# Strassen's seven products for the first layer of the last two experts, weight tiles in one pool, logit penalties in pairs

## The chip, the cores and the metric

The kernel runs on one core of a Trainium2 chip. The metric is device microseconds (us) of one execution of the whole program, as a median over runs; one further execution was profiled. PE is the matrix engine (PEld its weight loads), DVE the vector engine, ACT the scalar engine, POOL the general engine whose queue also issues the indirect DMAs, SP the engine that issues plain DMAs.

## What is computed

```python
X = np.fft.rfft(x, axis=1)                      # x: 8 x 2496 x 256
y = np.fft.irfft(X * (filt_r + 1j*filt_i), n=2496, axis=1)
x = y.reshape(19968, 256)
logits = x @ w_gate                             # 8 experts
# greedy: over all (token, expert) in falling order of logit, a token takes the expert
# if it has none yet and the expert has fewer than 19968/8 = 2496 tokens
for e in range(8):
    h = np.maximum(x[mask_e] @ w1[e], 0.0)      # 256 -> 1024
    out[mask_e] = h @ w2[e]                     # 1024 -> 256
```

## The kernel before

The program has two parts. First the filter: transforms by matmuls, up to about 440 us; it writes the rows x to DRAM (`xs`) and keeps the logits in `lg`. Then the experts, from 448 us on. Which expert is served in which order is found by `Route`: eight phases, each of which fixes one more expert and its 2496 tokens (`phase`, `threshold`, `counts`), lists them (`places`) and so allows the weights of that expert to be loaded (`Ffn.weights`, indirect DMAs issued by POOL, L804) and its rows to be gathered (`Ffn.gather`, L823). While PE works on one expert, DVE, ACT and a few small matmuls (L567, L580, L764) work on the route of the next one. After each phase the logits of served experts are pushed down by `pen`: eight activations on ACT, one per expert, at L727.

**Precision.** Matmuls take fp32r operands. A value is held as a rounded high part and a low part, the rest; a product is made of three matmuls (high by high, high by low, low by high). The parts come from `nc.scalar.copy` (high) and a DVE subtraction (low): for weights in `split` (L816, L817; tiles `w0h`, `w0l`, `w1`), for the gathered rows in `turn` (L840, L841; tiles `xo`, `z`).

**One expert.** `Ffn.run` takes 2496 tokens in five groups g of 512 (the last has 448). First layer, `first(g, f)`: for each of 8 column blocks f of the weights, six matmuls of 512 columns into one PSUM bank `pz` (L859), 48 a group; then a ReLU on ACT (L865) for the high part and a `scalar_tensor_tensor` on DVE (L873, L876 in the last group, POOL at L869 in some) for the low part, both into a tile `hl`. Second layer, for each of four blocks t of 128 tokens: 8 pairs of matmuls, 512 and 256 columns (L913, L914), into `py`; then a copy on ACT (L923), an addition on POOL (L924) and an indirect DMA to `out` (L925). The last block of an expert has 64 tokens and takes 16 matmuls of 256 columns (L909). The second layer of group g and the first layer of group g + 1 alternate (`ORD`). `turn` makes the transposed rows of the next group from eight matmuls by a unit matrix (L837) in passing.

**Order of the work.** PE's order is the order of the program text (`manual_schedule`). For the other engines a scheduler in the compiler orders the instructions by its own model of time, so an instruction of ACT or DVE can stand earlier or later in its queue than in the text. Each engine's queue is then worked off in that order. The route is put between the matmuls by `Pump`: the matmul code yields an amount of time (`yield 0.65` for a quarter of a second layer), `Pump.feed` adds it to a clock, and a step of the route is written when its lag has passed. `pump.limit` says which phase may finish.

PSUM has eight banks: two for the route (`a`), two for `py` (`b`), four for `pz` and the transposes (`c`).

Of the kernel before, what the change touches and what calls it, by code (L numbers as in the profile page):

```python
# [7 lines left out]
F32, F32R = mybir.dt.float32, mybir.dt.float32r  # L8
# [8 lines left out]
S = B * G  # L17
CAP = N
# [8 lines left out]
V1, V1D, V2, V3, VP, I2, AC = 8, 0.5, 3, 2, -1, 5, 6.5  # L27
NP, NZ, MZ, NXO, ZB, NH = 5, 4, 8, 4, 2, 10

# [440 lines left out]
class Route:  # L470
# [10 lines left out]
    def setup(s):  # L481
# [34 lines left out]
        nc.gpsimd.memset(s.r[:, :8], float(CAP))  # L516
        s.tmp = t("tmp", [117, S, 8])
        s.iota, s.sidx = t("iota", [117, 512], F16), t("sidx", [128, 20])
        io = s.tmp.rearrange("p s e -> p (s e)")[:, :512]
        nc.gpsimd.iota(io, [[1, 512]], base=0, channel_multiplier=0, allow_small_or_imprecise_dtypes=True)  # L520
# [116 lines left out]
    def phase(s, ph):  # L637
# [22 lines left out]
        s.want()  # L660
        vc, need, tot, mem = v("vc", [128, 1]), v("need", [128, 1]), v("tot", [117, 4]), v("m0", [117, S])
        tb, pf = v("tb", [117, 2], F16), v("pf", [117, 4])
# [6 lines left out]
        if ph < 7:  # L669
# [14 lines left out]
            nc.vector.scalar_tensor_tensor(q, s.desc, vc, r1[:, :8], op0=OP.is_equal, op1=OP.mult, accum_out=need)  # L684
            ga, eqm, cum = v("ga", [117, S]), v("eqm", [117, S]), v("cum", [117, S])
            nc.vector.scalar_tensor_tensor(ga, s.M, T[:117, :1], s.ar, op0=OP.is_gt, op1=OP.mult)
# [37 lines left out]
        if ph == 7:  # L724
            return
        for e in range(8):
            nc.scalar.activation(s.lg[:, :, e], s.lg[:, :, e], AF.Identity, bias=pen[:117, e:e+1], scale=1.0)  # L727
        with s.tc.issue_after(s.last):
            t, t3 = v("u", [117, S]), v("u2", [117, S])
            nc.vector.scalar_tensor_tensor(s.asg, mem, 50.0, s.asg, op0=OP.mult, op1=OP.add)  # L730
# [53 lines left out]
class Ffn:  # L784


    def __init__(s, tc, i, xs, out, cp, ww, zp, ps):
        s.tc, s.nc, s.xs, s.out, s.ww, s.zp, s.ps = tc, tc.nc, xs, out, ww, zp, ps
        s.w1 = i['w1l']
        s.w2 = i['moe_w2'].rearrange("e (q f) d -> (e q) (f d)", f=8)  # L790
        s.id = cp.tile([128, 128], F32, name="id")
        make_identity(s.nc, s.id)
        s.scat = []
        s.wt, s.xg, s.xT = {}, {}, {}

    def weights(s, e, widx):
        nc = s.nc
        raw = [s.ww.tile([128, 2048], F32, name=f"wr{k}", bufs=1) for k in range(2)]
        off = bass.IndirectOffsetOnAxis(ap=widx[:, :1], axis=0)
        hl = [[s.ww.tile([128, 2048], F32R, name=f"w0{h}", bufs=2) for h in 'hl']]  # L800
        s.w2b = s.ww.tile([128, 2, 2048], F32R, name="w1", bufs=2)
        hl.append([s.w2b[:, k] for k in range(2)])
        s.wt[e] = (raw, hl, s.w2b)
        s.load = lambda k: nc.gpsimd.indirect_dma_start(out=raw[k], out_offset=None, in_=(s.w1, s.w2)[k], in_offset=off).ins  # L804

    def split(s, e, part):

        nc = s.nc
        raw, hl, _ = s.wt[e]
        k, h = divmod(part, 4)  # L810
        src, (hi, lo) = raw[k], hl[k]
        if k == 0:
            h, j = divmod(h, 2)
            h += 2 * j
        src, hi, lo = (t[:, 512*h:512*h+512] for t in (src, hi, lo))
        nc.scalar.copy(hi, src)  # L816
        nc.vector.tensor_tensor(lo, src, hi.bitcast(F32), op=OP.subtract)  # L817

    def gather(s, e, g, ids):
        for t in range(4*g, 4*g + 4):  # L820
            n = min(128, CAP - 128*t)
            xg = s.xg[e, t] = s.wp.tile([128, D], F32, name="xg", bufs=8)
            s.lastg = s.nc.gpsimd.indirect_dma_start(out=xg[:n], out_offset=None, in_=s.xs,  # L823
                                           in_offset=bass.IndirectOffsetOnAxis(ap=ids[0][:n, t:t+1], axis=0)).ins

    def turn(s, e, g, h):
# [14 lines left out]
        return nc.vector.tensor_tensor(lo, p[:, :, :w], hi.bitcast(F32), op=OP.subtract).ins  # L841

    def run(s, e, pump, hook):

        nc = s.nc
        ids = pump.out[e]
        out_rows = s.out
        _, ((w1h, w1l), (w2h, w2l)), w2 = s.wt[e]
        hs = {}

        def first(g, f):
# [4 lines left out]
            for k in range(2):  # L856
                sl = slice(1024*k+128*f, 1024*k+128*f+128)
                for w, x in ((w1h, xh), (w1h, xl), (w1l, xh)):
                    nc.tensor.matmul(p[:, :n], w[:, sl], x[:, k, :n], start=m == 0, stop=m == 5)  # L859
                    m += 1  # L860
                yield 0.65 * n / 512
            hl = s.wp.tile([128, 1024], F32R, name="hl", bufs=NH)
            hs.setdefault(g, []).append(hl)
# [14 lines left out]
        def firsts(g, count):  # L878
            for f in range(len(hs.get(g, ())), min(8, len(hs.get(g, ())) + count)):
# [7 lines left out]
                yield from first(g, f)  # L887

        hook(('g', 1))
        for g in range(5):  # L890
            n = min(512, CAP - 512*g)
            yield from firsts(g, 8)
            if g == 4:
                hook('last')
            if g == 0:
                hook('w2')
            for t in range(4):
                if g < 4:
                    yield from firsts(g + 1, ORD[t])
                w = min(128, n - 128*t)  # L900
                half = w == 64
                pp = s.ps.tile([128, 2, D], F32, name="py", tag="b", bufs=2)
                p = pp[:, 0]
                hi, lo, both = slice(128*t, 128*t+w), slice(512+128*t, 512+128*t+w), slice(384, 512)
                m = 0
                for f in range(8):
                    if half:
                        for a, b in ((both, w2h), (hi, w2l)):
                            nc.tensor.matmul(p[:a.stop-a.start], hs[g][f][:, a], b[:, 256*f:256*f+256],  # L909
                                             start=m == 0, stop=m == 15, skip_group_check=True)  # L910
                            m += 1
                    else:
                        nc.tensor.matmul(pp, hs[g][f][:, hi], w2[:, :, 256*f:256*f+256], start=f == 0, stop=False, skip_group_check=True)  # L913
                        nc.tensor.matmul(pp[:, f % 2], hs[g][f][:, lo], w2h[:, 256*f:256*f+256], start=False, stop=f > 5, skip_group_check=True)  # L914
                    if f in ((3,) if half else (1, 3, 5)):
                        yield 0.65
                yy = s.wp.tile([128, 2, D], F32, name="y", bufs=4)
                y = yy[:, 0]
                if half:
                    nc.scalar.copy(y[:w], p[w:])  # L920
                    nc.vector.tensor_tensor(y[:w], p[:w], y[:w], op=OP.add)
                else:
                    s.lasta = nc.scalar.copy(yy, pp).ins  # L923
                    nc.gpsimd.tensor_tensor(y, y, yy[:, 1], op=OP.add)  # L924
                st = nc.gpsimd.indirect_dma_start(  # L925
                    out=out_rows, out_offset=bass.IndirectOffsetOnAxis(ap=ids[1][:w, 4*g+t:4*g+t+1], axis=0),
                    in_=y[:w], in_offset=None)
                for o in s.scat:
                    s.tc.declare_no_dep(st.ins, o.ins, reason="each token has one place")
                s.scat.append(st)  # L930
                if t in (1, 2) and g == 4:
                    hook(t)
                yield 0.65


def emit(tc, i, out):
    nc = tc.nc
    with ExitStack() as st:
# [52 lines left out]
        def weights(e):  # L991
            W.weights(e, pump.out[e][2])
            W.load(0)
            if e:
                R.wdma = W.load(1)
            split.extend((e, p) for p in range(8))
        pump.on_w = weights
# [19 lines left out]
        zst.close()  # L1017
        W.wp = pool(st, "ffp", reuse_waits="tile")
        def gather(e, g):
            pump.until((e, g))  # L1020
            W.gather(e, g, pump.out[e])
# [11 lines left out]
        n = 0  # L1033
# [4 lines left out]
        with tc.manual_schedule(engines={mybir.EngineType.PE}):  # L1038
            for e in range(8):
                pump.limit = e + 1  # L1040
                def hook(what):
                    if what == 'w2':
                        flush(8)
                    elif isinstance(what, tuple):
                        gather(e, what[1])
                    elif e < 7:
                        if what == 'last':
                            gather(e + 1, 0)
                            flush(4)
                        else:  # L1050
                            W.turn(e + 1, 0, what - 1)
                for pe in W.run(e, pump, hook):
                    pump.feed(pe)
# [91 lines left out]
```

## Time and profile before

| what | us |
|---|---|
| median of 3 runs | 1469.07 |
| lowest and highest run | 1453.58, 1471.03 |
| the profiled execution | 1465.58 |
| its span, first to last instruction | 1463.8 |

The profiled execution lies 1.8 us above its span and 3.5 us below the median; the three runs are 17 us apart. The mean granted PE clock of the span was 0.982. A row's duration of a matmul has the time through the array in it, so matmuls that follow each other overlap: the time that one costs is read as the distance of two starts.

### The profile page before, as it was taken

The page shows a single profiled execution, that of the slowest core. Times are in us where ns is not written, and L with a number is a line of the kernel's source. Part 1 is how long each engine was busy: PE and PEld are TensorE (multiplying, and loading weights), DVE is VectorE, ACT ScalarE, POOL GpSimd, SP SyncE. Part 2 cuts the span into 40 slices and gives each one's busy share as a digit, 9 for nine tenths or more (in the row PEclk, how much of TensorE's full clock was granted, in tenths as well). Part 3 has the DMA queues.
Part 4 walks back from the last instruction along what each step waited for, and adds up shares of the span by engine and source line. Part 5 has one row for each costly group of instructions (what it writes and reads, how often), then busy time and mean ns, then how long its engine had stood idle before and what let it go on. Part 6 is the DMA issues. An engine that isn't in the chain of part 4 may idle for free. (4 is left out here: it accounts for less than half of the span.)

```text
span 1463.8 us, 24844 instructions
## 1 busy us (share of the span) xinstructions
PE 1391.3 (95%) x9127; PEld 1148.7 (78%) x9127; DVE 955.6 (65%) x2574; ACT 723.7 (49%) x1686; POOL 663.6 (45%) x729
## 2 busy tenths in 40 slices
PE   7899999998997999899999899999999999999998
PEld 6889899776445787677778788787878888888887
DVE  5666676576566789666876976977877854432231
ACT  5666677534473345344544533644553654533332
POOL 5433344243004745553664546366545644445423
PEclk9999999999998999999999999999999999999999
DMA  8554454888892102112110211211211221111100
GB/s 263 185 148 143 126 163 116 237 239 206 328 348 74 51 22 95 53 35 75 59 52 25 98 49 39 90 51 48 95 37 50 102 95 52 38 48 46 42 26 27
DMA packets 54780, 149.17 MB, mean 102 GB/s; under 512 B 9258, under 2 KB 29866, under 8 KB 50706
## 3 DMA queue, kind: packets, MB, share of 16 engines
q0 software_dynamic: 17552, 57.72, 12.1%
q1 hardware_dynamic: 9803, 47.11, 10.6%
q10 hardware_dynamic: 27304, 42.76, 9.5%
q8 instruction: 72, 1.18, 0.3%
q14 instruction: 49, 0.40, 0.1%
HBM read 83.89 MB, written 63.70 MB: 101 GB/s over the span
## 5 line engine op out<-in xcount | busy, mean ns | idle before, releaser
L913 PE MATMUL py<-w,hl 128*128 128x512 f32 x1216 | 445.6, 405 | 0.5 <-ACT hl L865 0.3
L914 PE MATMUL py<-w,hl 128*128 128x256 f32 x1216 | 341.9, 281 | 1.0 <-DVE hl L873 0.6
L865 ACT ACTIVATE hl<-pz 128x512 fp32r<-128x512 f32 (+1 forms) x320 | 186.8, 586 | 214.7 <-PE pz L859 189.0
L859 PE MATMUL pz<-xo,w0h 128*128 128x512 f32 (+1 forms) x640 | 264.4, 413 | 10.3 <-DVE hl L876 3.7
L913 PEld LDWEIGHTS py<-w,hl 128*128 128x128 f32 x1216 | 229.8, 189 | 51.4 <-issue 1.2
L924 POOL TENSOR_TENSOR y<-y 128x256 f32<-128x256 f32 x152 | 122.4, 806 | 311.2 <-ACT y L923 309.9
L859 PE MATMUL pz<-xo,w0l 128*128 128x512 f32 (+1 forms) x640 | 249.9, 390 | 0.0
L859 PE MATMUL pz<-z,w0h 128*128 128x512 f32 (+1 forms) x640 | 249.3, 390 | 0.2 <-issue 0.2
L914 PEld LDWEIGHTS py<-w,hl 128*128 128x128 f32 x1216 | 230.7, 190 | 5.3 <-DVE hl L873 2.2
L873 DVE SCALAR_TENSOR_TENSOR hl<-pz,hl 128x512 fp32r<-128x512 f32 x227 | 155.0, 687 | 116.0 <-ACT hl L865 101.8
L823 POOL DMA_INDIRECT xg<-xs,xid x160 | 168.3, 1052 | 135.8 <-issue 41.0
L923 ACT COPY y<-py 128x512 f32<-128x512 f32 x152 | 89.1, 586 | 282.8 <-PE py L914 188.5
L925 POOL DMA_INDIRECT out<-y,oid x160 | 174.5, 1090 | 48.1 <-POOL y L924 33.6
L859 PEld LDWEIGHTS pz<-xo,w0h 128*128 128x128 f32 x640 | 122.0, 191 | 33.7 <-DVE hl L873 3.8
L232 POOL TENSOR_TENSOR P<-P 128x256 f32<-128x256 f32 x80 | 58.9, 737 | 184.6 <-DVE P L230 184.5
L859 PEld LDWEIGHTS pz<-xo,w0l 128*128 128x128 f32 x640 | 121.3, 190 | 24.1
L859 PEld LDWEIGHTS pz<-z,w0h 128*128 128x128 f32 x640 | 122.0, 191 | 17.3 <-DVE z L841 1.0
L216 ACT COPY Y<-p 64x240 f32<-64x240 f32 (+1 forms) x304 | 116.0, 382 | 30.4 <-PE p L209 19.8
L209 PE MATMUL p<-cS,xr 117*128 117x120 f32 x688 | 100.5, 283 | 7.2 <-DMA xr<-xl 7.1
L559 DVE TENSOR_TENSOR Gm<-M,thr 117x1232 bf16<-117x1232 f32 (+2 forms) x80 | 105.5, 1329 | 0.2
L209 PEld LDWEIGHTS p<-cS,xr 117*128 117x128 f32 x688 | 91.0, 199 | 11.2 <-issue 4.7
L224 PE MATMUL p<-cW,Y 128*128 128x128 f32 x640 | 88.7, 281 | 2.3 <-ACT Y L216 1.5
(229 smaller groups left out, 2274.2 us busy)
## 6 DMA issues: line engine op xcount, KB each, us to landing
zd<-zt ACTq DMA_DIRECT2D x80, 256.0 KB
z<-zd SPq DMA_DIRECT2D x18, 600.0 KB
xs<-xo ACTq DMA_DIRECT2D x18, 600.0 KB
xr<-xl SPq DMA_DIRECT2D x6, 1404.0 KB
xr<-xl SPq DMA_DIRECT2D x7, 1111.5 KB
xr<-zd SPq DMA_DIRECT2D x8, 600.0 KB
xs<-xr ACTq DMA_DIRECT2D x8, 600.0 KB
xs<-Y ACTq DMA_DIRECT2D x6, 600.0 KB
```

The costliest lines, as they stand in the source:

```text
L209: nc.tensor.matmul(p[:, q-q0, :120], s.xr[b][:, q], s.cS1, start=True, stop=True)
L216: x = (nc.vector.tensor_copy if dve else nc.scalar.copy)(dst, src)
L559: nc.vector.tensor_tensor(Gm[:, s0:s1, :m], s.M[:, s0:s1].unsqueeze(2).to_broadcast([117, s1 - s0, m]), thr[:117].unsqueeze(1).to_broadcas ...
L823: s.lastg = s.nc.gpsimd.indirect_dma_start(out=xg[:n], out_offset=None, in_=s.xs, in_offset=bass.IndirectOffsetOnAxis(ap=ids[0][:n, t:t+1] ...
L859: nc.tensor.matmul(p[:, :n], w[:, sl], x[:, k, :n], start=m == 0, stop=m == 5)
L865: s.lasta = nc.scalar.activation(h[:, :n], p[:, :n], AF.Relu).ins
L873: nc.vector.scalar_tensor_tensor(l[:, :n], p[:, :n], 0.0, h[:, :n].bitcast(F32), op0=OP.max, op1=OP.subtract)
L913: nc.tensor.matmul(pp, hs[g][f][:, hi], w2[:, :, 256*f:256*f+256], start=f == 0, stop=False, skip_group_check=True)
L914: nc.tensor.matmul(pp[:, f % 2], hs[g][f][:, lo], w2h[:, 256*f:256*f+256], start=False, stop=f > 5, skip_group_check=True)
L923: s.lasta = nc.scalar.copy(yy, pp).ins
L924: nc.gpsimd.tensor_tensor(y, y, yy[:, 1], op=OP.add)
L925: st = nc.gpsimd.indirect_dma_start(out=out_rows, out_offset=bass.IndirectOffsetOnAxis(ap=ids[1][:w, 4*g+t:4*g+t+1], axis=0), in_=y[:w], i ...
```

## The change

1. **Experts 6 and 7** (`E0 = 6`) take their first layer by Strassen's algorithm. A group's product (weights 1024 x 256, rows 256 x 512) is split in two on each of its three axes. Seven products of half size take the place of eight: `11·b11`, `12·b21`, `s1·t1`, `s2·t2`, `s3·t3`, `s4·b22`, `22·t4`, where s1 to s4 are sums of weight quarters and t1 to t4 sums of row quarters. Each is again three matmuls, now of 256 columns. `step` does half of the output columns (d), so a group has 2 x 42 matmuls. Sums of products are made in PSUM: a bank is copied into another by ACT (L939), DVE adds into a bank (L945) or to SBUF (L949), and matmuls go on accumulating in it.
2. `sums` makes the seven weight operands, `turns` the seven row operands.
3. `run7` takes the place of `run` for these experts: after each of four parts of a step come two quarters of the second layer of the group before (`s.pend`), which is held over from group to group and from expert to expert. Eight matmuls of ones (L1059) stand at the end of expert 5's first layers; the last group has 512 columns with zero rows (a `memset` of `xg`).
4. Weights of all experts lie in tiles `w0` of one size, 16 of them (before: `w0h`, `w0l` and `w1`, two each). `hl` (10) becomes `ha` (5) and `hb` (6). Some route tiles have one buffer instead of two.
5. After every second of the eight activations of `pen` there is a `yield`, and after phase 6 they are left out.
6. The yields of the second layer are 0.7 (0.45 in the block of 64) instead of 0.65.

```diff
+E0 = 6
...
-        for e in range(8):
+        if ph == 6:
+            yield 'd', 0.5
+        for e in range(8 if ph < 6 else 0):
             nc.scalar.activation(s.lg[:, :, e], s.lg[:, :, e], AF.Identity, bias=pen[:117, e:e+1], scale=1.0)
+            if e % 2 == 1 and e < 7:
+                yield 'd', 1.4
...
+    def sums(s, e):
+
+        r11, r21, r12, r22 = (s.wt[e][0][0][:, 512*h:512*h+512] for h in range(4))
+        tt = s.nc.vector.tensor_tensor
+        s.halve(*s.block(e, '11'), r11)
+        s1 = s.ww.tile([128, 1024], F32, name="w0", bufs=16)[:, :512]
+        tt(s1, r21, r22, op=OP.add)
+        yield
+        s.halve(*s.block(e, 's1'), s1)
+        tt(r21, r21, r11, op=OP.subtract)
+        yield
+        tt(r11, s1, r11, op=OP.subtract)
+        s.halve(*s.block(e, 's2'), r11)
+        yield
+        s.halve(*s.block(e, '12'), r12)
+        tt(r12, r12, r11, op=OP.subtract)
...
+        p = bank(0)
+        nc.scalar.copy(f[:, 0:4:3], p.rearrange("p (k c) -> p k c", c=256))
...
+        p = bank(1)
+        nc.scalar.copy(f[:, 1], p[:, 256:])
+        tt(f[:, 0], p[:, :256], f[:, 0], op=OP.subtract)
+        tt(f[:, 2], p[:, :256], f[:, 1], op=OP.subtract)
+        u2, u4 = tile(), tile()
+        s.halve(u4[:, 0, :256], u4[:, 1, :256], p[:, 256:])
+        tt(f[:, 1], f[:, 1], f[:, 0], op=OP.subtract)
+        s.halve(u2[:, 0], u2[:, 1], s.scr[:, :512])
+        tt(f[:, 3], f[:, 3], f[:, 1], op=OP.subtract)
...
+        p11, pm = bank(), bank()
+        prods((p11, '11', 'b11', True), (pm, 's1', 't1', True))
+        pu = bank()
+        nc.scalar.copy(pu, p11)
+        m5, c22 = (s.wp.tile([128, 512], F32, name="hr", bufs=2) for _ in range(2))
+        nc.scalar.copy(m5, pm)
+        yield 1.42
+        prods((pu, 's2', 't2', False), (p11, '12', 'b21', False))
+        p12 = bank()
+        nc.vector.tensor_tensor(p12, pu, m5, op=OP.add)
+        relu(p11, 0, 0)
+        yield 1.42
+        prods((pu, 's3', 't3', False), (p12, 's4', 'b22', False))
+        nc.vector.tensor_tensor(c22, pu, m5, op=OP.add)
+        yield 1.42
+        relu(p12, 1, 0)
+        relu(c22, 1, 1)
+        prods((pu, '22', 't4', False))
+        relu(pu, 0, 1)
+        yield 0.71
...
+                ps = [s.ps.tile([128, 512], F32, name="pz", tag="c", bufs=4) for _ in range(4)]
+                for n, m in ((512, True), (1, False)):
+                    for p in ps:
+                        nc.tensor.matmul(p[:, :n], s.ones16[:117], s.iota[:, :n], start=m, stop=True, skip_group_check=True)
...
-                    if f in ((3,) if half else (1, 3, 5)):
-                        yield 0.65
+            if m in (1, 3, 5):
+                yield 0.45 if half else 0.7
```

On ACT, in the route's third phase, these rows stand around the eight activations of `pen` (L727) before; `pz` banks are ReLUed into `hl`, `py` copied to `y`, `ptr` holds transposed rows:

```order
L923 COPY y_7831<-py_7795 128x512
L865 ACTIVATE hl_7890<-pz_7883 128x512
L923 COPY y_7910<-py_7893 128x512
L727 ACTIVATE lg_69<-lg_69,pen_7881 117x176 x8
L865 ACTIVATE hl_7921<-pz_7914 128x512
L840 CAST xo_7924<-ptr_7926 128x2x256
L865 ACTIVATE hl_7940<-pz_7933 128x512
```

In the changed program the activations of the same phase are at L731:

```order
L1016 ACTIVATE hb_8003<-pz_7996 128x512
L1016 ACTIVATE ha_8013<-pz_8006 128x448
L731 ACTIVATE lg_69<-lg_69,pen_7978 117x176 x3
L982 COPY y_8034<-py_8017 128x512
L731 ACTIVATE lg_69<-lg_69,pen_7978 117x176 x5
L982 COPY y_8073<-py_8050 128x512
```

One copy stands between three and five of them; in the phase after, one copy between one and seven, and in the second, fifth and sixth phase all eight follow each other, as before.

On PE, in the first group of expert 6, a bank of the first layer before is:

```order
L909 MATMUL py_14651<-w1_12366,hl_14560 64x256
L859 MATMUL pz_14680<-xo_14614,w0h_13829 128x512
L859 MATMUL pz_14680<-z_14615,w0h_13829 128x512
L859 MATMUL pz_14680<-xo_14614,w0l_13830 128x512
L859 MATMUL pz_14680<-xo_14614,w0h_13829 128x512
L859 MATMUL pz_14680<-z_14615,w0h_13829 128x512
L859 MATMUL pz_14680<-xo_14614,w0l_13830 128x512
```

In the changed program this is the second half (d = 1) of that group, and the start of the next group; products `11`, `s1`, `s2`, `12`, `s3`, `s4`, `22` in this order, six matmuls each:

```order
L925 MATMUL pz_14806<-z_14626,w0_14522 128x256 x6
L890 MATMUL ptr_14824<-id_4814,xg_14649 128x128 x2
L890 MATMUL ptr_14824<-id_4814,xg_14651 128x128 x2
L925 MATMUL pz_14819<-z_14626,w0_14527 128x256 x6
L925 MATMUL pz_14805<-xo_14615,w0_14530 128x256 x6
L890 MATMUL ptr_14853<-id_4814,xg_14653 128x128 x2
L890 MATMUL ptr_14853<-id_4814,xg_14655 128x128 x2
L925 MATMUL pz_14819<-z_14634,w0_14534 128x256 x6
L925 MATMUL pz_14848<-xo_14627,w0_14537 128x256 x6
L925 MATMUL pz_14819<-z_14634,w0_14540 128x256 x6
L925 MATMUL pz_14917<-z_14830,w0_14517 128x256 x6
L925 MATMUL pz_14918<-xo_14861,w0_14522 128x256 x6
```

The second layer of expert 5 is used up by then and that of this group needs both halves, so only transposes stand between the products here; in every later group quarters of a second layer stand there.

On DVE, at the same place, the queue before has a ReLU's low part, a low part of weights or rows, and the route in turn:

```order
L817 TENSOR_TENSOR w0l_14689<-wr0_14686,w0h_14688 128x512
L841 TENSOR_TENSOR z_14734<-ptr_14735,xo_14733 128x2x256
L873 SCALAR_TENSOR_TENSOR hl_14751<-pz_14742,hl_14751 128x512
L765 TENSOR_TENSOR loc_14698<-sidx_3687,rt_14758 128x2
L873 SCALAR_TENSOR_TENSOR hl_14768<-pz_14754,hl_14768 128x512
L817 TENSOR_TENSOR w0l_14689<-wr0_14686,w0h_14688 128x512
L841 TENSOR_TENSOR z_14734<-ptr_14771,xo_14733 128x2x256
```

In the changed program, from the addition into p12 (L945) on; `wr0_14938` is the raw first-layer weight of expert 7, `w0_15434` and the like its operands, `tmp` the scratch of the row sums:

```order
L945 TENSOR_TENSOR pz_14848<-pz_14819,hr_14821 128x512
L897 TENSOR_TENSOR z_14830<-tmp_3685,z_14830 128x512
L816 TENSOR_TENSOR w0_15434<-wr0_14938,w0_15434 128x512
L816 TENSOR_TENSOR w0_15529<-wr0_14938,w0_15529 128x512
L949 TENSOR_TENSOR hr_14822<-pz_14819,hr_14821 128x512
L816 TENSOR_TENSOR w0_15601<-wr0_14938,w0_15601 128x512
L934 SCALAR_TENSOR_TENSOR ha_14850<-pz_14805,ha_14850 128x512
L841 TENSOR_TENSOR wr0_14938<-wr0_14938 128x512
```

and further, to the low part of t1 and t2 (`xo_14861`) that the last PE row above reads:

```order
L901 TENSOR_TENSOR tmp_3685<-ptr_14853,tmp_3685 128x256
L902 TENSOR_TENSOR tmp_3685<-ptr_14853,tmp_3685 128x256
L934 SCALAR_TENSOR_TENSOR hb_14899<-pz_14848,hb_14899 128x512
L934 SCALAR_TENSOR_TENSOR hb_14902<-hr_14822,hb_14902 128x512
L934 SCALAR_TENSOR_TENSOR ha_14911<-pz_14819,ha_14911 128x512
L905 TENSOR_TENSOR tmp_3685<-tmp_3685 128x256
L816 TENSOR_TENSOR z_14862<-ptr_14853,z_14862 128x256
L907 TENSOR_TENSOR tmp_3685<-tmp_3685 128x256
L816 TENSOR_TENSOR xo_14861<-tmp_3685,xo_14861 128x512
```

The weight operands of expert 7, which the text makes in groups 2 to 4 of expert 6, stand in its first group.

## Rows read from the trace of the kernel before

**Rows 1.** The page: busy time and share of each engine.
```profile
PE 1391.3 (95%) x9127; PEld 1148.7 (78%) x9127; DVE 955.6 (65%) x2574; ACT 723.7 (49%) x1686; POOL 663.6 (45%) x729
```

**Rows 2.** Windows of experts 0, 6 and 7: length, busy us (instructions) by engine, clock, DMA.
```profile
448.00:583.00 135.00, 128.39 (x738) 103.84 (x739) 110.96 (x295) 62.76 (x144) 68.40 (x64) 0.97 0.17 58
1229.50:1345.70 116.20, 116.17 (x623) 98.08 (x622) 47.07 (x122) 52.03 (x117) 53.16 (x60) 1.00 0.14 45
1345.70:1458.70 113.00, 113.00 (x595) 96.62 (x592) 32.70 (x57) 38.72 (x68) 43.57 (x50) 1.00 0.11 36
```

**Rows 3.** Timeline of PE, expert 7, full group: start, duration, engine, line, shapes.
```profile
1355.64 0.39 PE L859 MATMUL pz<-xo,w0h 128*128 128x512 f32 x1
...
1357.91 0.39 PE L859 MATMUL pz<-z,w0h 128*128 128x512 f32 x1
```

**Rows 4.** Timeline of PE, expert 7, last group.
```profile
1437.11 0.37 PE L859 MATMUL pz<-xo,w0h 128*128 128x448 f32 x1
...
1438.33 0.39 PE L913 MATMUL py<-w,hl 128*128 128x512 f32 x1
```

**Rows 5.** Timeline of PE and PEld, the last block of 64 tokens.
```profile
1456.92 2.03 PE L909 MATMUL py<-w,hl 128*128 128x256 f32 x16
...
1456.81 1.89 PEld L909 LDWEIGHTS py<-w,hl 128*128 128x128 f32 x16
```

**Rows 6.** Groups by line and shape: count, busy us, mean ns, idle before.
```profile
L873 DVE SCALAR_TENSOR_TENSOR hl<-pz,hl 128x512 fp32r<-128x512 f32 x227 | 155.0, 687 | 116.0 <-ACT hl L865 101.8 <-issue 12.9 <-ACT junka L768 0.5
L876 DVE SCALAR_TENSOR_TENSOR hl<-pz,hl 128x384 fp32r<-128x384 f32 x64 | 35.0, 546 | 0.0
L817 DVE TENSOR_TENSOR w<-wr,w 128x512 fp32r<-128x512 f32 x32 | 21.7, 687 | 0.0
L865 ACT ACTIVATE hl<-pz 128x512 fp32r<-128x512 f32 x256 | 152.1, 597 | 178.4 <-PE pz L859 154.6 <-PE rt L580 7.8 <-issue 5.6
L859 PEld LDWEIGHTS pz<-xo,w0h 128*128 128x128 f32 x640 | 122.0, 191 | 33.7 <-DVE hl L873 3.8 <-ACT junka L768 2.2 <-DVE z L841 2.2
L1015 PE MATMUL rest<-iota,ones 117*128 117x512 f16 x24 | 5.3, 379 | 0.0
```

**Rows 7.** Timeline, expert 7: from the end of a bank to ReLU and low part.
```profile
1356.78 0.39 PE L859 MATMUL pz<-xo,w0l 128*128 128x512 f32 x1
...
1357.17 0.60 ACT L865 ACTIVATE hl<-pz 128x512 fp32r<-128x512 f32 x1 [1.36 <-PE pz L859]
...
1357.81 1.45 DVE L873 SCALAR_TENSOR_TENSOR hl<-pz,hl 128x512 fp32r<-128x512 f32 x2 [1.27 <-ACT hl L865]
...
1359.27 0.28 PE L914 MATMUL py<-w,hl 128*128 128x256 f32 x1
...
1359.62 0.28 PE L914 MATMUL py<-w,hl 128*128 128x256 f32 x1
```

**Rows 8.** Timeline of ACT and PE around the penalties of the third phase.
```profile
675.43 4.36 ACT L727 ACTIVATE lg<-lg,pen 117x176 f32<-117x176 f32 x8 [0.19 <-DVE pen L696]
...
678.89 0.40 PE L859 MATMUL pz<-xo,w0l 128*128 128x512 f32 x1
681.05 0.97 PE L837 MATMUL ptr<-id,xg 128*128 128x128 f32 x4 [1.76 <-DVE tab L718]
...
682.54 0.63 PE L859 MATMUL pz<-z,w0h 128*128 128x512 f32 x1
682.97 0.63 PE L859 MATMUL pz<-xo,w0l 128*128 128x512 f32 x1
```

**Rows 9.** Window with that wait: length, busy us by engine, clock, DMA.
```profile
675.00:700.00 25.00, 23.24 (x117) 18.94 (x116) 18.88 (x60) 15.60 (x34) 8.49 (x10) 0.93 0.30 106
```

**Rows 10.** What PE waited for from 448 us on: us in total, times, longest.
```profile
PE rt L567 <- DVE ex L769: 7.3, 4, 2.7
PE rt L580 <- DVE X L577: 4.2, 5, 2.7
PE pz L859 <- DVE hl L876: 3.7, 2, 1.9
```

More of the change, by code (lines that the diff above doesn't have):

```diff
@@ new lines, in second @@
+    def second(s, e, g, t, H, order):
+        nc, ids, w2 = s.nc, s.pids[e], s.wt[e][2]
+        w = min(128, CAP - 512*g - 128*t)
+        half = w == 64
+        pp = s.ps.tile([128, 2, D], F32, name="py", tag="b", bufs=2)
+        p = pp[:, 0]
+        for m, f in enumerate(order):
+            hi, lo, both = H(t, f)
+            b = w2[f//2][:, :, 256*(f%2):256*(f%2)+256]
+            w2h, w2l = b[:, 0], b[:, 1]
+            if half:
+                nc.tensor.matmul(p, both, w2h, start=m == 0, stop=False, skip_group_check=True)
+                nc.tensor.matmul(p[:64], hi[:, :64], w2l, start=False, stop=m == 7, skip_group_check=True)
+            else:
+                nc.tensor.matmul(pp, hi, b, start=m == 0, stop=False, skip_group_check=True)
+                nc.tensor.matmul(pp[:, m % 2], lo, w2h, start=False, stop=m > 5, skip_group_check=True)
+            if m in (1, 3, 5):
+                yield 0.45 if half else 0.7
+        yy = s.wp.tile([128, 2, D], F32, name="y", bufs=4)
+        y = yy[:, 0]
+        if half:
+            nc.scalar.copy(y[:w], p[w:])
+            nc.vector.tensor_tensor(y[:w], p[:w], y[:w], op=OP.add)
+        else:
+            s.lasta = nc.scalar.copy(yy, pp).ins
+            nc.gpsimd.tensor_tensor(y, y, yy[:, 1], op=OP.add)
+        st = nc.gpsimd.indirect_dma_start(
+            out=s.out, out_offset=bass.IndirectOffsetOnAxis(ap=ids[1][:w, 4*g+t:4*g+t+1], axis=0),
+            in_=y[:w], in_offset=None)
+        for o in s.scat:
+            s.tc.declare_no_dep(st.ins, o.ins, reason="each token has one place")
+        s.scat.append(st)
+        yield 0.45 if half else 0.7
@@ L843, in run, with seconds @@
+    def seconds(s, e, g, H, order):
+        for t in range(4):
+            yield from s.second(e, g, t, H, order)
     def run(s, e, pump, hook):
         nc = s.nc
-        ids = pump.out[e]
-        out_rows = s.out
-        _, ((w1h, w1l), (w2h, w2l)), w2 = s.wt[e]
+        blk = s.wt[e][1]
         hs = {}
@@ L917, in run @@
[L917 to L927, printed above, removed]
@@ L995, in weights @@
                 R.wdma = W.load(1)
-            split.extend((e, p) for p in range(8))
+            split.extend((e, p) for p in range(8 if e < E0 else 0))
         pump.on_w = weights
```

190 lines of the change are left out of this document (144 added, 46 removed).

## The prediction

> **What bounds the kernel now.** I read the busy shares first, then the windows of the experts, then the timeline inside one expert, and last the list of waits. The shares put PE far ahead: 95% against 65% for DVE and 49% for ACT [rows 1]. [...] Expert 0, with the whole route beside it, takes 135.0 us at a clock of 0.97 and DVE busy for 111 [rows 2]: there the waits on the route count too.
>
> The timeline gives prices by distances of starts. Ten steps of 512 columns lie between 1355.64 and 1357.91: 0.227 us each [rows 3]. Six of 448 columns take from 1437.11 to 1438.33: 0.203 [rows 4]. The sixteen of 256 columns, each with a weight load of its own, span 2.03 us; less the 0.28 that one such record lasts [rows 7], over fifteen steps, this is 0.117 [rows 5]. Half the columns cost 52% and not half. A pair of the second layer costs 0.35, so a quarter, two pairs, 0.69 [rows 7].
>
> **The change part by part.** All terms are against the profiled execution, 1465.6 us.
>
> *Columns.* Before, two experts make 2 x 4 x 48 = 384 matmuls of 512 and 96 of 448: 384 x 0.227 + 96 x 0.203 = 106.7 us. After, 2 x 5 x 84 = 840 of 256: 98.3. One eighth fewer products, less 3% for the shorter matmuls and less the zero rows of the last group: **-8.4**. Second layer and transposes keep their number.
>
> [...]
>
> *Ones at the end of expert 5.* Four of 512 at 5.3/24 = 0.22 [rows 6] and four tiny ones: **+1.1**.
>
> *Steady steps.* A handoff has these parts: ACT starts 0.39 after the last matmul's start, about 0.2 after the next could have started; one piece takes 0.60 on ACT, 0.69 on DVE, with 0.04 between [rows 6, 7]. In a step, s2 ends, DVE adds p12 (0.2 + 0.69 = 0.9 later), and PE may go on with s3; meanwhile PE has product `12` (0.70) and two quarters (1.38). 2.1 against 0.9: 1.2 us, not quite two DVE pieces, may stand ahead. The handoff over c22 (L949) is alike. The copies on ACT have 0.70 + 1.38 from the end of `11`, and need 0.2 + 0.60. DVE's load per group: twelve pieces of 512 in the two steps, three in `turns`, five small ones of 256; with 0.69, and 0.41 for 256 (drawn on from 687 and 546 ns for 512 and 384 [rows 6]), 12.4 us, of about 22 that PE has (9.9 + 0.9 + 11.0). It fits: **0**. The bounds are below nothing by nothing (PE cannot go faster than its columns) and above by 36 us, the third rival.
>
> *The first group of expert 6.* Here the cover is missing: no quarter stands between the products of d = 1, only transposes (the PE piece of the order). And the DVE queue there carries the weight sums of expert 7, put forward by the scheduler. From L945 to the low part that the next group's second product reads there are 16 pieces behind L945: 11 of 512 and 5 of 256, 11 x 0.69 + 5 x 0.41 = 9.6 us; L945 ends 0.9 after s2's end, so 10.5. PE meanwhile has `12` 0.70, transposes 0.43, s3 and s4 1.40, `22` 0.70, `11` 0.70 and one matmul 0.12: 4.05. PE waits 6.5, split over two or three places. Four of the pieces are expert 7's, 2.8 us. Before it, at expert 6's very first product, the row sums are late by some 0.5 (eight pieces after the last ReLU against ones and one block of second layer): **+7.0**. From both sides: 0, if the queue runs ahead of what I count, since the sums were ready early; and 10, if four more sums ahead of L945 (2.8) are late too.
>
> [...]
>
> *From expert 6 to 7.* In the last step of expert 6 the second-layer weights of expert 7 (four pieces) and two sums stand in the same queue. c22 then starts about 1.2 late and 4.5 us of DVE lie between it and t1's low part; with c22's own 0.69 that is 6.4 after s3 (0.2 included in the lateness), PE has 0.70 + 1.38 + 0.70 + 1.38 + 0.70 + 0.12 = 5.0: **+1.5** (0 to 3).
>
> *Penalties.* The block holds ACT for 4.36 us and once costs PE 1.76, since a ReLU behind it is late and DVE's queue with it; with the slow clock behind it, 3.5 [rows 8, 9]. The pairs are meant to let others in between. But the order shows them only in part: three and five with one copy between, one and seven, and eight in a row in three phases. The yields moved the text, not ACT's queue. I count nothing for the pairs and **-0.2** for the phase in which they are left out, whose ACT time was hidden. Bounds: -4 and +4, because such a block can fall on another ReLU.
>
> *Weight tiles, two kinds of hl, single buffers, yields.* The same instructions, with finer or equal releases, hidden behind PE's matmuls; the yields 0.7 put route steps earlier by 7% of a quarter, while waits on the route (L567, L580) cost 11.5 us today [rows 10]. **0**, from -5 to +11.
>
> Sum: 1465.6 - 8.4 + 1.1 + 7.0 + 1.7 + 1.5 - 0.2 = **1468**. The gain is real and is spent at the seams. The median shown is 3.5 above the profiled execution, but the three runs are 17 apart, so I add nothing.
>
> **Rivals.**
> - *No loss at the seams.* DVE has long idle times in expert 6 today [rows 2], and if the sums of expert 7 run before they stand in the way, the 7.0, 1.7 and 1.5 go: 1458. Against it: queues are in order, and 16 pieces are 16 pieces.
> - *Route waits grow.* Earlier route steps find DVE not done; 11.5 us of waits [rows 10] double: 1480. For it: DVE is busy for 111 of 135 us beside expert 0 [rows 2]; against it, the lags have slack in later experts.
> - *Slower: the handoffs of each step fail.* Place: L945 and L949 in every step, 40 in all. It decides from the point where three pieces instead of one or two stand ahead of them: 0.2 + 3 x 0.69 + 0.69 against 2.1, 0.9 late each: 36 us, 1504. For it: row sums and ReLUs share this queue, and in expert 6 the route too. Against it: 12.4 of 22 us.
> - *Slower: weight loads not hidden.* If a 256-column matmul costs its weight load's 0.191 [rows 6]: 840 x 0.191 = 160, 62 more than 98.3: 1530. Sixteen in a row at 0.117 [rows 5] speak against it; they are few, and the seven products also switch banks.
> - *Faster.* Of PE's waits, 11.5 on the route and some 10 more with the slow clock behind them vanish in the first six experts, with no loss at the seams: 1458 - 21 = 1437. The pairs not being in ACT's order speaks against it.
> - *The change does not do what it says* holds for the pairs, as the order shows, and is in the sum.
>
> **How the numbers follow.** Main case 0.55, no loss at the seams 0.24, route 0.11, handoffs 0.05, weight loads 0.02, faster 0.03. Against 1469.07, within 2% (29 us, about what a measurement of this kernel can tell from no change) lie the main case, the seams and the route: 0.90. Slower 0.07, faster 0.03. The range takes in 1458 and 1480 with some of the spread of runs: 1452 to 1482.
>
> **What would show it.** Right: matmuls of 256 columns in experts 6 and 7 about 0.117 apart; expert 7 near 113.0 - 4.2 + 1.5 = 110 us; a wait of several us on DVE at the second product of expert 6's second group, with a slow clock behind it; blocks of eight penalties still there. Wrong: waits in every step of expert 7; a distance near 0.19; or an undisturbed start of expert 6. The forecast fails if the end moves by over 29 us either way.

## The result, and the profile after

The changed kernel takes 1467.0 us (median of 20 runs, 1452.82 to 1480.45), the kernel before 1455.45 in 20 runs beside it: the ratio is 1.0075, 95% interval 1.0053 to 1.0097. It leaves out runs over 1.5% above the fastest of their kernel (three of the 20 after), so it lies a little under that of the medians. The change costs 11 us, 8 to 14 by the interval. Forecast were 1468.0 us, no change against the 1469.07 shown. That the time came out 1 us from the one named is luck, since two errors cancelled: the base was 10 us high, and the loss, put at 2.4 us over it, was 9 short.

The profiled execution of the changed kernel is its fastest of the 20, 1452.82 us. All of the 12.8 us that it is shorter than the profile of before lies ahead of the first expert: the experts' first matmul starts at 435.0 instead of 448.2 us, though PE's 3372 matmuls are the same up to there. So the experts alone are to be compared, and both kernels were profiled once more, unchanged: there the start came at 445.6 and 454.3. The page's shares of the first profile after answer to [rows 1]:

```profile
PE 1379.1 (95%) x9495; PEld 1154.1 (80%) x9495; DVE 1009.1 (70%) x2676; ACT 765.1 (53%) x1768; POOL 681.2 (47%) x735
```

> The kernel before once more, for a second profiled execution. 'Sum': experts 2 to 7 in 733 to 735 us; the part ahead of the first expert anywhere between 435 and 455, as in the profiles of kernels that are the same up to there. The waits of 2.9 us each at 588 and 598 us in expert 1, which no other kernel with the old route shows, are of one execution and not of the kernel, or come back.

> The changed kernel once more, unchanged, for a second profiled execution. The one at hand is the fastest of its 20 (1452.8 us), its part ahead of the first expert 11 to 20 us shorter than in the others. Theory 'sum': its experts cost what the two parts cost apart, 3.5 us (Strassen, experts 5 to 7) and 5 us (route, experts 2 to 5), 8 to 9 us over before, and the rest of the measured 11 is spread: experts 2 to 7 in 742 to 745 us again (743.2 in the first profile, 734.0 in before). Rival 'unseen': something else costs 3 us more in a usual execution: 747 or more.

Measured: before 1.0005 (0.9979 to 1.0032) of itself, the changed kernel 1.0084 (1.0054 to 1.0114). Experts 2 to 7 took 733.3 us in before, as 'sum' had it, and 745.4 in the changed kernel, just above what 'sum' allowed and under the 747 of 'unseen'. Windows of experts 0 to 4 and of 5 to 7, columns as in [rows 2]; first the second profile of before, then that of the changed kernel:

```profile
454.30:1108.90 654.60, 634.08 (x3858) 517.51 (x3859) 515.56 (x1519) 307.15 (x705) 354.57 (x335) 0.99 0.18 58
1108.90:1457.90 349.00, 348.47 (x1899) 293.94 (x1897) 154.46 (x425) 148.49 (x313) 157.51 (x174) 1.00 0.17 53
```
```profile
445.60:1106.30 660.70, 635.71 (x3835) 516.58 (x3836) 507.38 (x1517) 310.02 (x711) 361.77 (x338) 0.99 0.17 58
1106.30:1460.90 354.60, 345.62 (x2290) 307.86 (x2289) 221.29 (x549) 186.97 (x393) 167.04 (x177) 0.99 0.16 53
```

The first window ends with the last matmul of expert 4's block of 64 tokens, the second with that of expert 7's. Between these two profiles 6.1 us are lost in experts 0 to 4, where only the route's edits and the tiles changed, and 5.6 in experts 5 to 7, 11.7 together. But the two lie at the ends of a spread: the first profile of the changed kernel has 657.0 and 353.9 us. Against means over the kernels below (655.7 with the old route, 349.2 without either part) its two profiles lose 3 and 5 us, so some 8 of the 11 are found in the experts; the rest is open and within the interval. In the last window PE is busy for 2.9 us less and yet it is longer: what Strassen's layer saves is lost again in waits. In the first profile of before, experts 0 to 4 took 661.6 us, 7 more than in its second: two waits of 2.9 us each in expert 1, at 588 and 598 us, came at that length in none of the other kernels with the old route. The forecast took them for the kernel's own.

What PE waited for from 435 us on in the first profile after, as [rows 10]:

```profile
PE ptr L870 <- DVE ha L1024: 4.0, 4, 2.4
PE pz L925 <- ACT xo L815: 3.6, 1, 3.6
PE rt L582 <- DVE X L579: 3.3, 5, 1.3
...
PE rt L569 <- DVE Gm L561: 1.8, 3, 1.0
PE ptr L870 <- DMA xg<-xs,xid: 1.7, 1, 1.7
```

The waits of the two route matmuls that [rows 10] names (here L569, L582) are 5.1 us, where it had 11.5, 5.4 of them the two waits above. In their place PE waits for ReLUs' low parts (the first row, transposes that need a free bank), once for Strassen's row sums (L925), and once for gathered rows to land (the last row).

### The profile page after: what moved, and what is told of

It reads as the page before. It is cut to its first block, busy times and chain, and to the rows that moved or that the text cites. A ratio compares the mean times of both kernels' runs of the same rounds, so it can differ in the third digit from the quotient of the medians.

```text
span 1451.0 us, 25790 instructions
## 1 busy us (share of the span) xinstructions
PE 1379.1 (95%) x9495; PEld 1154.1 (80%) x9495; DVE 1009.1 (70%) x2676; ACT 765.1 (53%) x1768; POOL 681.2 (47%) x735
## 4 chain that ended last, share of the span: by engine, by line
PE 58%; DVE 12%; DMA 4%; ACT 2%; issue 2%; POOL 1%; ACTq 0%; POOLq 0%; DVEq 0%
PE pz L1010 18%; PE py L972 17%; PE py L973 8%; PE pz L925 6%; PE pv L396 2%; PE rt L569 2%; PE ptr L870 1%; DMA xs<-xo 1%; DVE w L816 1%; DMA zd<-zt 1%; DVE Gm L561 1%; PE rt L770 1%; DVE ha L1024 1%; DVE OH L764 1%; DVE tmp L648 1%
## 5 line engine op out<-in xcount | busy, mean ns | idle before, releaser
L1010 PE MATMUL pz<-xo,w 128*128 128x512 f32 (+1 forms) x960 | 337.6, 406 | 7.6 <-DVE hb L1024 2.6
L972 PE MATMUL py<-w,ha 128*128 128x512 f32 x616 | 248.4, 412 | 0.1
L972 PE MATMUL py<-w,hb 128*128 128x512 f32 x600 | 233.3, 397 | 0.0
L1010 PEld LDWEIGHTS pz<-xo,w 128*128 128x128 f32 x960 | 183.7, 191 | 45.9 <-DVE hb L1024 3.3
L1010 PE MATMUL pz<-z,w 128*128 128x512 f32 (+1 forms) x480 | 189.0, 394 | 2.3 <-DVE loc L771 1.8
L973 PE MATMUL py<-w,ha 128*128 128x256 f32 x616 | 173.3, 281 | 0.3 <-DVE ha L1027 0.3
L973 PE MATMUL py<-w,hb 128*128 128x256 f32 x600 | 169.2, 282 | 3.1 <-DVE hb L1027 2.9
L972 PEld LDWEIGHTS py<-w,ha 128*128 128x128 f32 x616 | 117.0, 190 | 21.6 <-issue 0.5
L972 PEld LDWEIGHTS py<-w,hb 128*128 128x128 f32 x600 | 112.9, 188 | 24.9
L973 PEld LDWEIGHTS py<-w,ha 128*128 128x128 f32 x616 | 117.4, 191 | 2.6 <-DVE ha L1027 1.0
L973 PEld LDWEIGHTS py<-w,hb 128*128 128x128 f32 x600 | 113.5, 189 | 4.9 <-DVE hb L1027 3.9
L1010 PEld LDWEIGHTS pz<-z,w 128*128 128x128 f32 x480 | 92.2, 192 | 15.3 <-DVE z L874 3.7
```

The costliest lines, as they stand in the source:

```text
L972: nc.tensor.matmul(pp, hi, b, start=m == 0, stop=False, skip_group_check=True)
L973: nc.tensor.matmul(pp[:, m % 2], lo, w2h, start=False, stop=m > 5, skip_group_check=True)
L1010: nc.tensor.matmul(p[:, :n], w1[:, i], x[:, k, :n], start=m == 0, stop=m == 5)
```

## The experiments

Each ratio is of runs on one chip with before beside them; "0-4" and "5-7" are the lengths of the two windows in the one profile of each. A sum of the two is good to 3 to 7 us: the two profiles of before have 1010.5 and 1003.6, those of the changed kernel 1010.9 and 1015.3, tiles_only 1006.5 at a ratio of 1.0004. So means count for more: in experts 0 to 4 the seven profiles with the old route (before's first, with its two waits, left out) have 654.6 to 656.8, in mean 655.7, and the four with both route edits (after twice, route_only, held_sums) 657.0 to 660.7, in mean 658.6. In experts 5 to 7, before twice and tiles_only have 348.9 to 349.7, in mean 349.2. "Loss" below is what PE's starts lie further apart than the usual distance after a matmul of that form, added up over a window.

| kernel | ratio (95% interval) | 0-4 | 5-7 |
|---|---|---|---|
| before, second | 1.0005 (0.9979 to 1.0032) | 654.6 | 349.0 |
| after, second | 1.0084 (1.0054 to 1.0114) | 660.7 | 354.6 |
| tiles_only | 1.0004 (0.9970 to 1.0037) | 656.8 | 349.7 |
| strassen_only | 1.0028 (0.9996 to 1.0060) | 655.6 | 353.1 |
| route_only | 1.0023 (0.9994 to 1.0052) | 658.7 | 350.9 |
| pairs_only | 1.0046 (1.0016 to 1.0075) | 654.8 | 353.8 |
| pace_only | 1.0048 (1.0017 to 1.0078) | 663.5 | 348.6 |
| pairs_quarter | 1.0020 (0.9999 to 1.0042) | 653.1 | 350.9 |
| true_pairs | 1.0140 (1.0112 to 1.0169) | 667.6 | 353.6 |
| held_sums | 1.0081 (1.0050 to 1.0111) | 657.9 | 355.7 |
| pool_held | 1.0070 (1.0035 to 1.0106) | 655.8 | 359.3 |
| pool_cover | 1.0108 (1.0060 to 1.0156) | 656.6 | 358.2 |
| placed | 1.0030 (1.0006 to 1.0053) | 655.2 | 352.2 |
| last_only | 1.0006 (0.9978 to 1.0034) | 655.3 | 347.8 |

### The parts of the change apart

Each is the changed kernel with lines put back. No Strassen is

```diff
-E0 = 6
+E0 = 9
```

the old pace `yield 0.65` for 0.7 and 0.45 in the second layer, the old penalties the loop without yields in all phases. route_only has the first, tiles_only all three, strassen_only the last two (the old pace in experts 0 to 5 only).

> No Strassen, penalties in one block again in all phases, yields 0.65 again: only the weight tiles, the two kinds of hl tiles, the single route buffers and the wider scratch are left of the change. 'Seams' and 'route' both: 1455, the time of before. A rival 'tiles' (finer releases or single buffers cost DVE or ACT a wait): 1460 or more.

> All eight experts by the old first layer (no Strassen); weight tiles, single buffers, penalties with yields and the 0.7 yields stay as in the changed kernel. Median of before 1455, of the changed kernel 1467, so 12 us are to be found. Theory 'seams': what the last two experts lose at their seams (7.5 us in the window from 1225 us, 3.2 in that from 1325, against 8.4 saved in columns) and what follows carries the loss: this kernel stands at before, 1455, within 4. Rival 'route': the moved route and penalties cost 9 to 12 us in experts 0 to 5, and Strassen's layer comes out even: 1464 to 1467.

> Strassen in experts 6 and 7 with the weight tiles, but penalties in one block in all phases and the old yields (0.65) in experts 0 to 5. 'Seams': all of the loss is left, 1464 to 1468. 'Route': the loss is gone, 1452 to 1457.

The tiles cost nothing that the runs show (at most 0.4% by the interval). Strassen alone is 1.0028, the route alone 1.0023; neither carries the loss by itself, so both theories fall as they were put. By the profiles, against the means, Strassen costs 3.9 us in experts 5 to 7 (353.1 against 349.2) and the route 3.0 in experts 0 to 4 and 1.7 in 5 to 7, where some 24 of its matmuls have moved: 8.6 in all, about what the changed kernel loses there. Each interval alone reaches no change; that the changed kernel's 1.0075 and 1.0084 lie above the upper ends of both (1.0060 and 1.0052) speaks for a cost of each part on top of the other. Experts 5 to 7 in tiles_only and strassen_only:

```profile
1103.10:1452.80 349.70, 349.29 (x1899) 294.02 (x1898) 154.17 (x425) 148.69 (x313) 156.59 (x173) 1.00 0.16 53
```
```profile
1108.20:1461.30 353.10, 344.69 (x2267) 307.28 (x2264) 213.00 (x531) 189.46 (x399) 162.63 (x175) 0.99 0.16 53
```

PE has 4.6 us less to do, DVE 59 more and ACT 41.

### Why the route's edits cost

> No Strassen, old yields of 0.65 in the second layer, but the penalties with their yields in pairs and left out in phase 6, on the new weight tiles. In the profiles so far experts 2 to 5 take 504.6 us with none of the route's edits and 509.8 with both. Theory 'pairs': the yields between the penalties put each phase of the route off, and the 5 us are theirs: 509 to 510 here, 505 in the run with the pace alone. Rival 'pace': the yield of 0.7 costs them: 505 here, 510 there. End: 5 us or 0 above the kernel with the tiles alone (1459 in the last comparison, where before had 1460).

> No Strassen, penalties in one block as before, but yields of 0.7 in the second layer (and four of 0.45 in the block of 64 tokens), on the new weight tiles. 'Pairs': experts 2 to 5 in 505 us, end as before within 3. 'Pace': 509 to 510, end 3 to 6 later.

Both cost alone, so neither theory holds: experts 2 to 5 take 513.3 us with the pairs and 507.6 with the pace, 504.6 with neither. Together they cost rather less than either (1.0023, though the intervals overlap). What they move is the lead of the route: how long before the end of an expert the fourth gather for the first rows of the next is issued. Timeline of POOL, the first and the last of the four for expert 1, in before (second profile; expert 0 ends at 591.4) and after (first profile; 567.5), and what DVE and PE do there after:

```profile
569.32 0.98 POOL L823 DMA_INDIRECT xg<-xs,xid  x1 [1.85 <-DVE t1b L778]
...
573.12 2.55 POOL L823 DMA_INDIRECT xg<-xs,xid  x1 [0.30 <-issue]
```
```profile
554.17 0.98 POOL L856 DMA_INDIRECT xg<-xs,xid  x1 [4.13 <-DVE t L782]
...
557.96 0.95 POOL L856 DMA_INDIRECT xg<-xs,xid  x1 [0.31 <-issue]
...
566.07 2.16 DVE L650 TENSOR_TENSOR tmp<-tmp,val 117x1408 f32<-117x1408 f32 x1
567.61 0.40 PE L1010 MATMUL pz<-xo,w 128*128 128x512 f32 x1
...
569.11 0.68 DVE L874 TENSOR_TENSOR z<-ptr,xo 128x512 fp32r<-128x512 f32 x1
569.84 0.50 PE L1010 MATMUL pz<-z,w 128*128 128x512 f32 x1 [1.83 <-DVE loc L771]
```

The lead is 18.3 us before and 9.5 after, and after, expert 1's second matmul waits 1.83 for its low part (L874, done at 569.79; the `loc` that the row names is a short operation behind it). The rows themselves are there: PE has transposed them by 565.5. Their low part stands on DVE behind a long pass of the route (L650). For experts 1, 2, 3 the leads are 18.3, 25.3, 31.7 in before; 9.5, 13.7, 22.5 after; 9.3, 8.2, 8.3 with the pairs alone; 19.2, 30.7, 44.8 with the pace alone. The yields between penalties make every later step of the route due later, the yield of 0.7 makes the clock run faster, so that steps are written earlier. With the first, route passes on DVE fall on the start of the next expert, and its second group's rows can land late (PE waits 1.7 to 3.0 us for them in the three profiles of the changed kernel and route_only, in neither profile of before). With the second, PE meets route steps that DVE has not done: its waits on the route's matmuls are 10.8 us with the pace alone, up to expert 5, and 7.8 in tiles_only; the rest of that loss is not traced. With the pairs alone the experts 2 and 3 begin with losses of 2.2 us each, at 709.8 and 838.5, again behind L650. Over all kernels, the starts of experts 1 to 5 with a lead under 10 us lose 2.1 us or more in their first 3 us, those with 17 or more at most 0.8, but for one of the waits in the first profile of before; in between it is 0.6 to 2.4. The route's edits also gain: expert 0 takes 133 us with both, where the old route takes 137 to 139, and it is experts 1, 2 and 4 that lose more than that.

> As with the pairs alone (no Strassen, yields of 0.65 in the second layer), but the three yields between the penalties ask for 0.35 instead of 1.4 each. Theory 'lead': what costs is that each phase of the route comes later; the last of the four gathers for an expert's first group is issued 18.4, 25.0 and 31.5 us ahead of experts 1, 2 and 3 without the pairs and 9.3, 8.2 and 8.3 with them. With a quarter of the yields the leads should come back to 15 to 18, 20 to 25 and 24 to 32, the waits of 2.2 us at the starts of experts 2 and 3 go, and experts 2 to 5 take 504 to 508 us (504.6 without pairs, 513.3 with them). Rival 'cut': the cuts in the text between the penalties, however short, cost by another order on the engines: 511 to 514.

> No Strassen, yields of 0.65; the penalties with their yields as in the changed kernel, and each held behind the last ReLU of the text, so that ACT's queue has them really in pairs with ReLUs and copies between. In all kernels so far they ran as eight in one go for 4.4 to 4.95 us, pairs or not. Theory 'clock of the route': the yields cost by putting the route off (each phase 1.4 x 3 later), not by the order of ACT: experts 2 to 5 stay near the 513 us of the pairs that are pairs in the text alone. Rival 'block': true pairs take away the waits behind the block (1.9 + 0.7 us in expert 1, 2.6 + 0.5 and 1.6 in the changed kernel) and experts 2 to 5 fall to 506 or less.

With a quarter of the yields the leads are 14.8, 15.5, 23.2. Experts 2 to 5 still take 511.2 us, which is the rival's number; but that window was ill chosen, since the route's work moved between experts 0, 1 and the rest: over experts 0 to 5 it is 774.0, with the pairs 778.6, in before 774.4. The ratio, 1.0020, lies between as well, with an interval that overlaps that of the pairs. I take the delay as the main cause; that is argued from the leads, and that the cuts cost nothing is not shown. true_pairs changes ACT's queue:

```diff
-            nc.scalar.activation(s.lg[:, :, e], ...)
+            with s.tc.issue_after(s.ffn.lasta) if ... else ExitStack():
+                nc.scalar.activation(s.lg[:, :, e], ...)
```

Now the penalties beside the experts run in twos, with other work of ACT between, and it is by far the slowest, 1.0140: expert 2 alone begins with a wait of 4.7 us, on the low part of its first rows. Experts 2 to 5 take 525.6 us, so neither theory's number came. Against 'block': the eight in a row were not the dearest thing. But the leads are shorter still (9.2, 6.2 and 7.1), so the order on ACT is not tested apart from the delay. In the changed kernel the penalties do run nearly in a row. Timeline of ACT and PE at the block of the fourth phase, as [rows 8] show that of the third:

```profile
786.43 0.62 ACT L731 ACTIVATE lg<-lg,pen 117x176 f32<-117x176 f32 x1 [3.27 <-DVE pen L698]
...
787.42 3.84 ACT L731 ACTIVATE lg<-lg,pen 117x176 f32<-117x176 f32 x7
...
791.16 0.57 ACT L1016 ACTIVATE ha<-pz 128x512 fp32r<-128x512 f32 x1
...
792.51 0.78 PE L870 MATMUL ptr<-id,xg 128*128 128x128 f32 x4 [2.44 <-DVE ha L1024]
```

One and seven, 4.8 us; a ReLU stands behind them, and PE waits 2.44 for its low part, as it does in route_only. In before no loss over 0.3 us lies behind the block of this phase (799.9 us). The block costs by where it falls, and the yields moved it.

### Why Strassen's layer does not gain

The end of the first group of expert 6, timeline of DVE, ACT and PE after:

```profile
1223.77 0.70 DVE L945 TENSOR_TENSOR pz<-pz,hr 128x512 f32<-128x512 f32 x1
...
1224.97 1.28 DVE L816 TENSOR_TENSOR w<-wr,w 128x512 fp32r<-128x512 f32 x2
...
1226.91 1.68 PE L925 MATMUL pz<-z,w 128*128 128x256 f32 x12 [0.68 <-DVE hr L949]
...
1227.98 0.68 DVE L841 TENSOR_TENSOR wr<-wr 128x512 f32<-128x512 f32 x1
...
1231.04 0.41 DVE L905 TENSOR_TENSOR tmp<-tmp 128x256 f32<-128x256 f32 x1
...
1231.54 1.23 ACT L815 CAST xo<-tmp 128x512 fp32r<-128x512 f32 x2 [1.81 <-DVE tmp L905]
...
1232.21 0.38 PE L925 MATMUL pz<-xo,w 128*128 128x256 f32 x1 [3.62 <-ACT xo L815]
```

Eight weight pieces for expert 7 run on DVE from 1219 to 1229 us, the L816 and L841 above among them, ahead of the row sum (L905); ACT casts its result from 1231.54 on, and PE has waited 3.62. held_sums takes these sums out of there, by `with s.tc.issue_after(s.lasta): next(s.todo)`.

> The changed kernel, with the weight sums of expert 7 held behind the last ReLU ahead of them in the text, so that they are no longer put forward into the first group of expert 6 (four pieces of 0.68 us between 1219 and 1229 us). 'Seams': 3 to 6 us of the 7.5 in that window go, 1461 to 1464, and the wait on u2's high part there shrinks from 3.6 us to under 1.5. 'Route': no change beyond 3 us, 1464 to 1467.

The loss in the window from 1225 us falls from 7.5 to 3.1, as forecast for 'seams'; but the end is no earlier. The pieces now run at the seam to expert 7, which loses 7.0 instead of 3.2. Timeline there:

```profile
1329.08 2.82 DVE L816 TENSOR_TENSOR w<-wr,w 128x512 fp32r<-128x512 f32 x3
...
1332.48 1.28 DVE L816 TENSOR_TENSOR w<-wr,w 128x512 fp32r<-128x512 f32 x2
...
1334.55 0.41 DVE L905 TENSOR_TENSOR tmp<-tmp 128x256 f32<-128x256 f32 x1
...
1335.72 0.38 PE L925 MATMUL pz<-z,w 128*128 128x256 f32 x1 [2.35 <-ACT z L815]
```

The next two give the fifteen weight operations of expert 7 to POOL (on strassen_only; `eng = s.nc.gpsimd` in the sums and the split; the sums held as above), the second with two quarters after each piece of the first group instead of four and none.

> Strassen in experts 6 and 7 with the route as before, and all weight sums and low parts of expert 7 (15 operations of 128x512) computed on POOL, each held to its place in the text. Theory 'DVE queue': what is lost in the first group of expert 6 (7.3 us in that window) and at the seam to expert 7 (2.4 and 1.4) is the queue of DVE, and goes with its 15 x 0.68 us: experts 5 to 7 in 353.1 us with the sums on DVE, here 345 to 348, and the end 3 to 6 under before. Rival 'missing cover': the waits are those of one handoff without second-layer matmuls to hide it, whoever makes the sums: 351 to 354, the end 3 to 5 over before.

> The same as the one with the sums on POOL, and in the first group of expert 6 two quarters of the second layer after each piece instead of four and none, so that its second step has two covers more. 'DVE queue': no change by this, 345 to 348 us for experts 5 to 7. 'Missing cover': 2 to 3 us less than the kernel without it, and no wait above 1 us left in that group.

Both theories fail by their numbers: 359.3 and 358.2 us. But for the first group of expert 6 'DVE queue' holds: with the sums on POOL only two waits are left there, of 0.8 and 1.0 us, the same as in held_sums, and the cover changes neither. The loss went to the seam, where DVE, freed of the sums, was stopped by POOL (pool_held):

```profile
1330.85 5.58 DVE L902 TENSOR_TENSOR tmp<-tmp 128x256 f32<-128x256 f32 x1
...
1331.17 4.98 POOL L812 TENSOR_TENSOR w<-wr,w 128x512 fp32r<-128x512 f32 x4
...
1337.19 0.58 PE L922 MATMUL pz<-z,w 128*128 128x256 f32 x1 [3.57 <-ACT z L811]
```

A DVE operation of 0.41 us lasts 5.58, until POOL's four are done. Two more put the DVE pieces where there seems to be room, or ask for fewer. placed holds one sum to a step from the second group on (`g > 0`, as in held_sums) and expert 7's second-layer weights to its own first group; last_only is strassen_only with `E0 = 7`.

> Strassen in experts 6 and 7, route as before; the weight sums of expert 7 on DVE again, one to a step from the second group of expert 6 on and held to that place, and the four second-layer weights of expert 7 held to its own first group, so that neither stands in the first group of expert 6 nor at the seam. Theory 'DVE queue': the 6 us lost in the first group of expert 6 and the 3 lost at the seam shrink to 2 and 2; experts 5 to 7 take 346 to 349 us (353.1 with the sums put forward, 349.6 without Strassen), the end 0 to 4 under before. Rival 'moved, not removed': each piece of DVE work delays a handoff wherever it stands, as with the held sums (1.5 us in the fourth group and 7.0 at the seam): 352 to 355, the end 3 to 6 over before.

> Strassen in expert 7 alone (starting group 7 instead of 6), route as before. Half the columns saved (4.2 to 4.7 us), the ones once (1.1); no other expert's sums behind it. 'DVE queue': the first group loses 2 to 3 us as where the sums were held, experts 5 to 7 in 348 to 350 us, as without Strassen. Rival 'missing cover': the first group loses its 6 to 7 us here too, 352 to 354.

placed loses 3.7 us in the first group and 1.4 at the seam, but 6.2 in the first group of expert 7, where the second-layer weights now stand: moved, not removed, and 352.2 us. last_only loses no more at its start than held_sums did (0.8 and 1.0 us of waits) and gains 1.2 us in the window; its ratio, 1.0006, is not told from before. No version here beats the kernel before.

## Why the prediction was right or wrong

- *What bounds* held: a busy PE in experts 6 and 7 (106.3 of 113.2 and 111.3 of 111.9 us in the profile after), and DVE's queue where it waits (3.62 us at the end of the first group, with the eight weight pieces ahead of the row sum).
- *Columns*, -8.4: right. The 256-column matmuls follow each other at 0.118 us (six of L925 from 1347.72 to 1348.43 are 0.71), and a steady group of expert 7 takes 22.05 us, where it took 23.17. The rival of 1530, with weight loads that are not hidden, is out: a load at L925 lasts 0.188 us from 1354 us on, more than that distance.
- *Ones*, +1.1: right; from the first of them at 1204.31 to the matmul behind them at 1205.36 it is 1.05.
- *Steady steps*, 0: right; from 1354 us to the end the list of waits is empty. The rival of 1504 is out.
- *First group of expert 6*, +7.0, +1.7 for the clock behind its wait, *seam* +1.5: the window from 1225 us loses 7.5, with the tiles alone 1.1, so 6.4 for the first two; the place and the queue are as told. No run shows the 1.7 by itself. What the profile after shows behind the wait of 3.62 us is a granted clock of 0.50 from 1234 to 1236 us, with four pairs of the second layer 0.64 us apart from 1233.88 on instead of 0.35, 1.2 us more for the four, and 0.93 over the window (in the first profile of before the clock was 0.50 from 682 to 684 us, behind the wait of [rows 8]):

```profile
1225.00:1250.00 25.00, 20.36 (x134) 18.43 (x133) 15.78 (x37) 13.41 (x31) 8.66 (x10) 0.93 0.12 36
```

  The window of the seam loses 3.2 where before lost 0.7. So this part of the sum, -8.4 + 1.1 + 7.0 + 1.7 + 1.5 = +2.9, measured +3.9 in experts 5 to 7 (strassen_only, 353.1 against a mean of 349.2).
- *Penalties -0.2, yields 0*: this step failed. It was right that the pairs hardly appear in ACT's queue. But "The yields moved the text, not ACT's queue" left out what else they move: the time at which every later step of the route is due, and so where its passes stand in DVE's queue. The bound of +11 was kept, but the value was not 0: 4.7 by the windows of route_only against the means, 3.3 by its ratio (interval -0.9 to 7.6), and each edit alone is clear of no change (1.0046 and 1.0048). The rival *route waits grow* comes near it, but by steps that come earlier: so it is with the pace alone (1.0048). In the changed kernel the pairs outweigh the pace, and the steps come later.
- *The base*: 1465.6 was taken as it stood, 10 us above the median of 20 runs. 5.8 us of it were two waits in expert 1 that its second profile does not show ([rows 10] holds them as the longest of L567 and L580, 2.7 each; the second profile has 4.9 us in 3 waits and 1.8 in 5 there, up to expert 5); the other 4 are not traced. Added to a sum that was 9 us short, they gave nearly the time measured. Of those 9, the route is 3 to 5 and Strassen's part 1; the rest lies in no stretch that the profiles tell apart.

## What to carry to other kernels

Before a saving on the bounding engine is counted, follow the work that it puts on the next engine's queue: here 8.4 us of columns cost 59 us of DVE, and pieces held back from one seam stood in the next. A yield in a planner moves every later step: measure by how much (the lead of the gathers here) and what the moved steps then stand ahead of, not only which instructions change places. And take a base from two profiles or from stretches that several kernels share, where runs spread by 1%.

## What the runs showed of the hardware that was not expected

POOL stopped a DVE operation with both operands in SBUF: 5.58 us for 0.41 above. It ended at 1336.43, 0.28 us behind the last of the four POOL operations (1336.15), so DVE came in at none of the gaps between them. The first profile after has the same on a smaller scale: the same operation (L905) took 0.41 to 1.32 us from 1092 us on, the 1.32 at 1322.50 beside a POOL addition of 0.74 at 1322.78. Operations that read PSUM kept their time there: the sums of L945 and L949 took 0.70 and 0.68 to 0.69 us in all 20 of each, one of L949 at 1309.38 for 0.69 beside a POOL addition of 0.73 at 1309.39.

The same kernel came to its experts at 435.0 and at 445.6 us (after), at 448.2 and 454.3 (before): 10.6 of the 15 us between the two profiled executions of the changed kernel lie there. The granted clock was 0.986 and 0.980 over the whole of these two; how much of it that explains, and what sets the rest, is open.
